# A kernel of slot attention and a GELU feed-forward net: the hand-written order of its start is laid out anew and reaches further

## The chip, the cores and the metric

The kernel runs on one core of one Trainium2 chip. The metric is the time of one execution in device microseconds. The kernel before took 703.89 us, the median of three runs (703.46 to 704.96). Five engines of the core matter here. TensorE (PE in the profile, PEld for its weight loads) does matrix products and transposes; VectorE (DVE) and ScalarE (ACT) do the work element by element; GpSimd (POOL) does some integer additions; SyncE (SP) issues the loads and stores. Each engine takes its instructions strictly in the order of its own queue.

## The reference

Eight batches, eight heads, 576 positions of 64 columns, 32 slots; then a feed-forward net over 4608 tokens with 512 inputs, 2048 hidden columns and 512 outputs.

```python
a = np.exp(phi - np.max(phi, axis=2, keepdims=True))       # softmax over the 576 positions
a = a / (np.sum(a, axis=2, keepdims=True) + 1e-09)
k_m = np.einsum('bhsm,bhsd->bhmd', a, k)                   # 32 slots of keys and of values
v_m = np.einsum('bhsm,bhsd->bhmd', a, v)
scores = scale * np.matmul(q, k_m.transpose(0, 1, 3, 2))
attn = np.exp(scores - np.max(scores, axis=-1, keepdims=True))
attn = attn / (np.sum(attn, axis=-1, keepdims=True) + 1e-09)
x = np.matmul(attn, v_m)                                   # heads side by side: 4608 x 512
h = x @ w_in
g = 0.5 * h * (1.0 + erf(h * inv_sqrt2))
return (g @ w_out).astype(np.float32)
```

## The kernel before

The kernel never forms `x`. For each batch it multiplies the 256 rows of slot values (8 heads of 32 slots) into `w_in` once; the result is `U`, 256 x 2048. The hidden layer is then `h = P U`, with `P` the attention weights of a token over all 256 slots. A batch is two halves of 288 tokens, and the 2048 hidden columns are 16 blocks of 128.

To keep float32's precision, each large product is made of three: an operand is split into a rounded part (`_hi`, a cast) and the remainder (`_lo`, a subtraction on VectorE), and hi x hi, lo x hi and hi x lo are summed. So each operand costs one cast and one subtraction: `U` (pieces `Uh`, `Ul`), the weights `p` (`n_hi`, `n_lo` in batch 0; `ph`, `pl` later), the GELU's output (`gh`, `gl`), and `w_out` (`dE`, `dF`). The casts can stand on VectorE or on ScalarE.

The weights come from memory as 64-bit floats and are decoded on the chip, block by block, 32 half blocks in all: `dB` (two steps on ScalarE, on tiles `y` and `raw`), `dC` and `dS` (VectorE, `y`), `dG` (VectorE, `raw`), `dDi` or `dDo` (GpSimd).

The stages of the start. `phi` of batch 0 is loaded (`Lphi`), its maximum taken (`amax`), exponentiated (`aexp`), and transposed on TensorE (`at`, tiles `pt`, copied by `atc` into `aT`). `slots` multiplies it with keys and values (tile `pk`); `km` scales the sums; `slotsT` transposes them (tile `tn`); `kT` copies them into `k_blocks` and `kT`. In batch 0 the scores are made in three parts (`n_score`, tiles `psc`, the third with half as many tokens), each with maximum, subtraction, exponential, sum, reciprocal and product (`n_max` to `n_mul`, tiles `mx`, `s`, `smx`); `n_T` transposes them back, and `n_hi` and `n_lo` split them into `p_hi` and `p_lo`, of which piece 0 serves the first half of tokens, and pieces 1 and 2 the second. `Up` makes a block of `U` (tile `pu`). `h.0.0.0` is the first hidden block of batch 0's first half, `gelu` its GELU, and `p.0.0` is the first projection, twelve matmuls into the tiles `acc`. Batches 0 and 1 then run through the first eight blocks while the weights are decoded, and batches 2 to 7 come later one after the other, in halves of tokens (`P`, `O`). For batches from 2 on, `phi` is loaded in its other layout as well (`Lphin`, straight into `aT`, which has one buffer), the maximum is brought there through memory (`mw`, `mr`), added (`anat`) and exponentiated. `W` is a filler: a matmul of ones whose result nobody reads.

What sets the order: `START` is a string of pieces, each with its arguments and, behind a colon, the engine of its copy (`d` VectorE, `a` ScalarE). The kernel walks through it and calls one function for each. After its last piece a plan of pieces with due times takes over (`put`, `run`), in a loop over the hidden blocks. At the end every instruction is tied behind the one before it on its engine, so this order is each engine's order. `HOME` gives each big tile its place in the on-chip memory, so a load waits until the last reader of what was there is done. In the page's line numbers, L210 is the helper of all copies, L531 `slots`, L560 `slots_T`, L615 `score_n`, L598 `u_p`, L693 `n_lo`, L855 `hidden`, L882 `gelu_lo`, L895 `products`.

## Time and profile before

| | |
|---|---|
| median of three runs | 703.89 us (703.46 to 704.96) |
| profiled execution, its own time | 704.61 us |
| its span in the trace | 702.8 us |
| mean granted clock of TensorE | 0.981 |
| TensorE busy | 691.1 us, 98% |
| VectorE busy | 388.6 us, 55% |
| ScalarE busy | 298.4 us, 42% |
| GpSimd busy | 46.6 us, 7% |

The rows below come from the profiled execution, in microseconds from the start of its span; 1.8 us of its time lie outside the span. A clock of 1.00 is 2.4 GHz, of 0.50 1.2 GHz. Matmuls follow each other in a pipeline, so the time of a group of them runs from the start of the first to the end of the last, and neighbours overlap.

### The profile page before, as it was taken

The numbers are of one execution on the slowest core, as the hardware profiler recorded it, in microseconds if no ns is written. First come the engines' busy times: TensorE is split into PE (matmuls) and PEld (weight loads), VectorE is DVE, ScalarE is ACT, GpSimd is POOL, SyncE is SP. The second block draws the span as 40 slices with busy tenths as digits, with TensorE's granted clock in tenths as the row PEclk, the third lists the DMA queues.
The fourth block names the chain that finished last, engine by engine and source line by source line (L and its number), as shares of the span: only waits on it lengthen the run. The fifth ranks groups of instructions, "written<-read, shape, count | busy, mean of one in ns | idle before, by whom it ended". The sixth has DMA issues, their size and how long they took to land.

```text
span 702.8 us, 12357 instructions
## 1 busy us (share of the span) xinstructions
PE 691.1 (98%) x4940; PEld 576.6 (82%) x4940; DVE 388.6 (55%) x705; ACT 298.4 (42%) x768; POOL 46.6 (7%) x39
## 2 busy tenths in 40 slices
...
GB/s 318 329 211 172 154 197 62 133 29 212 86 142 117 177 217 23 65 137 159 190 1 32 82 2 31 1 98 1 30 1 31 83 1 31 1 31 0 31 1 45
DMA packets 30716, 64.37 MB, mean 92 GB/s; under 512 B 3780, under 2 KB 8644, under 8 KB 30660
## 3 DMA queue, kind: packets, MB, share of 16 engines
...
q10 hardware_dynamic: 96, 0.13, 0.1%
q14 instruction: 17, 0.14, 0.1%
...
## 4 chain that ended last, share of the span: by engine, by line
PE 94%; DMA 1%; DVE 1%; SPq 0%; ACT 0%; issue 0%
PE acc L895 50%; PE h L855 29%; PE tacc L895 6%; PE pu L598 4%; PE psc L598 1%; PE psc L506 1%; DMA raw<-w_in 1%; PE pk L531 1%; PE x L506 1%; SPq L345 0%; PE pk L506 0%; PE psc L519 0%; PE psc L560 0%; DVE aT L210 0%; PE x L519 0%
## 5 line engine op out<-in xcount | busy, mean ns | idle before, releaser
L855 PE MATMUL h<-p_hi,U 128*128 128x288 f32 x1024 | 203.8, 298 | 0.0
L895 PE MATMUL acc<-wo_hi,gh 128*128 128x512 f32 x512 | 200.6, 392 | 0.0
L895 PE MATMUL acc<-wo_hi,gl 128*128 128x512 f32 x512 | 199.7, 390 | 0.0
L895 PE MATMUL acc<-wo_lo,gh 128*128 128x512 f32 x512 | 199.6, 390 | 0.0
L867 ACT ACTIVATE gf<-h 128x256 f32<-128x256 f32 x192 | 74.0, 387 | 265.0 <-issue 206.4
L855 PEld LDWEIGHTS h<-p_hi,U 128*128 128x128 f32 x1024 | 164.0, 188 | 23.0 <-issue 8.3
L210 DVE CAST gh<-gf 128x512 fp32r<-128x512 f32 x109 | 46.9, 430 | 167.4 <-ACT gf L867 165.3
L895 PEld LDWEIGHTS acc<-wo_hi,gh 128*128 128x128 f32 x512 | 96.5, 188 | 21.1 <-DVE gl L882 3.4
L895 PEld LDWEIGHTS acc<-wo_hi,gl 128*128 128x128 f32 x512 | 96.1, 188 | 21.5 <-DVE gl L882 0.9
L895 PEld LDWEIGHTS acc<-wo_lo,gh 128*128 128x128 f32 x512 | 96.1, 188 | 15.8
L855 PE MATMUL h<-p_lo,U 128*128 128x288 f32 x512 | 108.8, 294 | 0.1
L882 DVE TENSOR_TENSOR gl<-gf,gh 128x512 fp32r<-128x512 f32 x128 | 94.3, 736 | 15.2 <-ACT gh L210 5.7
L855 PEld LDWEIGHTS h<-p_lo,U 128*128 128x128 f32 x512 | 81.4, 188 | 0.6 <-DVE p_lo L693 0.6
L814 DVE TENSOR_TENSOR U<-pu,U 128x512 fp32r<-128x512 f32 (+2 forms) x50 | 40.8, 834 | 42.0 <-ACT U L210 41.8
L869 ACT ACTIVATE tails<-h 128x32 f32<-128x32 f32 x192 | 37.4, 195 | 0.0
L598 PE MATMUL pu<-w_in_sb,kT 64*32 64x512 f32 (+2 forms) x624 | 34.4, 528 | 0.4 <-ACT kT L210 0.4
L210 ACT CAST U<-pu 128x512 fp32r<-128x512 f32 (+2 forms) x42 | 30.4, 759 | 7.4 <-PE pu L598 7.3
L305 POOL TENSOR_TENSOR w_in_sb<-y,raw 128x512 int32<-128x512 int32 x16 | 23.8, 1493 | 43.8 <-DVE y L285 11.8
L305 POOL TENSOR_TENSOR y<-y,raw 128x512 int32<-128x512 int32 x16 | 21.9, 1374 | 56.5 <-DVE y L285 23.9
L272 ACT ACTIVATE y<-raw 128x512 f32<-128x512 f32 x32 | 21.6, 675 | 8.9 <-issue 4.3
L895 PE MATMUL tacc<-wo_hi,gh_t 128*128 128x512 f32 x64 | 25.0, 391 | 0.0
L895 PE MATMUL tacc<-wo_hi,gl_t 128*128 128x512 f32 x64 | 24.9, 389 | 0.0
...
## 6 DMA issues: line engine op xcount, KB each, us to landing
...
raw<-w_out SPq DMA_DIRECT2D x16, 512.0 KB, 5.6
raw<-w_in SPq DMA_DIRECT2D x16, 512.0 KB, 4.5
out<-o SPq DMA_DIRECT2D x16, 512.0 KB, 2.7
...
aT<-phiN SPq DMA_DIRECT2D x6, 512.0 KB, 4.7
...
```

The costliest lines, as they stand in the source:

```text
L210: return e.copy(dst, src) if e is nc.scalar else e.tensor_copy(dst, src)
L272: nc.scalar.activation(y, high.bitcast(F32), AF.Abs, scale=2.0**16)
L305: nc.gpsimd.tensor_tensor(w, y, low, op=ALU.add)
L506: nc.tensor.matmul(pk[32 * j : 32 * j + 32, : 2 * D], st["aT", b][:, c, g, 32 * j : 32 * j + 32], st["kv", b, g, c][:, :, j, :], start=(c ...
L531: nc.tensor.matmul(pk[32 * j : 32 * j + 32, w0 * D : (w0 + n) * D], st["aT", b][:rows, c, g, 32 * j : 32 * j + 32], t[:rows, w0 : w0 + n, ...
L598: nc.tensor.matmul(ps[g][M * j : M * j + M], st["kT", b][rows, t, M * j : M * j + M], moving[j][rows], start=True, stop=True,)
L814: nc.vector.tensor_sub(u[:, ..., 1, :], pu, u[:, ..., 0, :].bitcast(F32))
L855: i = nc.tensor.matmul(h[:, :HS], u[g][w], x[:, g, :], start=(n == 0), stop=(n == 3 * G - 1))
L867: nc.scalar.activation(gf[:, f % 2 * n : f % 2 * n + n], h[:, :n], AF.Gelu)
L869: nc.scalar.activation(t, h[:, n:HS], AF.Gelu)
L882: nc.vector.tensor_tensor(g_of("gl", *k), g_of("gf", *k), g_of("gh", *k).bitcast(F32), op=ALU.subtract)
L895: nc.tensor.matmul(acc, x, w[:, f, :], start=(first and n == 0), stop=(last and n == 2))
```

## The change

`START` grows from 694 pieces to 850 and is written in another order. Before, it ended in the last projections of batch 1's second eight blocks; now it reaches through the first half of batch 2's tokens (`P.2.0.7`, `O.2.0.1`). The plan behind it has the same entries less the pieces already done. `HOME` is unchanged. What each piece computes is unchanged too; the piece `anat` is taken apart into `aadd` (VectorE) and `ax` (ScalarE), which batches from 3 on had already, and the store of a finished pair of output tiles is a piece of its own (`os`) where it was the last step of `o`. The lines that set `far` stand ahead of the walk through `START`, so that pieces of batches 2 and later find them. Which engine makes a copy changes at some pieces: in the program VectorE has 690 instructions where it had 707, ScalarE 775 where it had 756; the others have as many as before.

The diff, of the table only its first and last lines:

```diff
-W.4.3 Lphi.0.0 amax.0.0 aexp.0.0 at.0.0.0 Lphi.0.1 amax.0.1 aexp.0.1 anorm.0 atc.0.0.0:d
...
-h.1.15.1 gelu.1.15.0 pl.2.1 p.1.14 gelu.1.15.1 gh.1.15 amax.3.1 gl.1.15 tg.1.0 p.1.15
+Lphi.0.1 Lphi.0.0 Lwo.0 Lkv0.0.0 Lkv0.1.0 Lq.0.0 W.4.3 amax.0.1 Lwo.1 W.4.13 amax.0.0 Lwi.0
...
+O.2.0.0:a h.2.1.1 O.2.0.1 gelu.2.0.1 gelu.2.1.1 Lkv.5.1.2 gh.2.1.0 gl.2.1.0
@@ -469,10 +480,6 @@
         c = {"tn": b - 1, "pk": 3 if b == 4 else b - 2}[what]
         psc = [(("psc", c, hf), g) for hf in range(2) for g in range(G)]
         return [cut(psc[g], FB - P, FB) for g in ((1, 2) if what == "tn" else (0, 3))]
-
-    def a_nat(b):
-        a_add(b)
-        a_x(b)
 
     def a_x(b):
         x = st["aT", b].rearrange("p c g n -> p (c g n)")[:, : S * G]
@@ -959,11 +966,12 @@
             nc.vector.tensor_add(o, a, st["part", b, j])
         else:
             copy("da"[j % 2], o, a)
-        if f == NF - 1 and j % 2:
-            r = b * S + (j - 1) * P
-            nc.sync.dma_start(
-                out[r : r + 2 * P, :].rearrange("(c p) n -> p c n", p=P), st["o", b, j // 2]
-            )
+
+    def store(b, j):
+        r = b * S + (j - 1) * P
+        nc.sync.dma_start(
+            out[r : r + 2 * P, :].rearrange("(c p) n -> p c n", p=P), st["o", b, j // 2]
+        )
 
     def tail_evict(b):
         o = sb.tile([P, DM], F32, **home(f"to_{b}"))
@@ -985,7 +993,7 @@
     pieces = {
         "Lphi": load_phi, "Lkv": load_kv, "Lkv0": load_kv0, "Lq": load_q,
         "Lwi": lambda f: load_w(0, f), "Lwo": lambda f: load_w(1, f),
-        "Lphin": load_phin, "mw": a_out, "mr": a_back, "anat": a_nat, "aadd": a_add, "ax": a_x, "amax": a_max, "aexp": a_exp, "anorm": a_norm,
+        "Lphin": load_phin, "mw": a_out, "mr": a_back, "aadd": a_add, "ax": a_x, "amax": a_max, "aexp": a_exp, "anorm": a_norm,
         "at": a_T, "atc": a_Tc, "slots": slots, "km": slots_m,
         "slotsT": slots_T, "kT": k_T,
         "n_score": score_n, "n_max": n_max, "n_sub": n_sub, "n_exp": n_exp, "n_sum": n_sum,
@@ -994,10 +1002,13 @@
         "ph": p_hi, "pl": p_lo, "Up": u_p, "Uh": u_h, "Ul": u_l, "U": absorb,
         "W": warm, "dB": dec_b, "dC": dec_c, "dG": dec_g, "dS": dec_s, "dDi": lambda f: dec_d(0, f),
         "dDo": lambda f: dec_d(1, f), "dE": dec_e, "dF": dec_f,
-        "h": hidden, "gelu": gelu, "gh": gelu_hi, "gl": gelu_lo, "p": project, "o": evict,
+        "h": hidden, "gelu": gelu, "gh": gelu_hi, "gl": gelu_lo, "p": project, "o": evict, "os": store,
         "P": project_half, "O": evict_half,
         "tg": tail_split, "tp": tail_project, "to": tail_evict,
     }
+    st.update({("far", "pu", b, f): 1 for b in range(3, B) for f in (4, 12)})
+    st.update({("far", "psc", b, 1): 1 for b in range(3, B)})
+    st.update({k: 1 for k in (("far", "xt", 3), ("far", "pu", 2, 12))})
     done = set()
 
     def do(x):
@@ -1032,7 +1043,7 @@
         put(t + 3, f"mw.{b}")
         put(tn - 1, f"Lphin.{b}")
 
-        put(tn + 1, f"anat.{b}", *(f"aexp.{b}.{g}" for g in range(G)), f"anorm.{b}")
+        put(tn + 1, f"aadd.{b}", f"ax.{b}", *(f"aexp.{b}.{g}" for g in range(G)), f"anorm.{b}")
 
 
     prepare(2, T2, T2 + 5)
@@ -1044,9 +1055,6 @@
     put(t + 13, "slotsT.2", "kT.2")
 
 
-    st.update({("far", "pu", b, f): 1 for b in range(3, B) for f in (4, 12)})
-    st.update({("far", "psc", b, 1): 1 for b in range(3, B)})
-    st.update({k: 1 for k in (("far", "xt", 3), ("far", "pu", 2, 12))})
     for hf, at in ((0, n + 22), (1, n + 26)):
         put(at - 4 if hf == 0 else n + 23, f"Lq.2.{hf}")
         put(at, f"score.2.{hf}", f"sT.2.{hf}.0", f"sT.2.{hf}.1")
@@ -1165,7 +1173,10 @@
         if b < 2:
             behind = [f"p.{step}"]
             if end:
-                behind += [f"o.{b}.{j}.{f}" for j in range(NT)]
+                for j in range(NT):
+                    behind += [f"o.{b}.{j}.{f}"]
+                    if f == NF - 1 and j % 2:
+                        behind += [f"os.{b}.{j}"]
         else:
             behind = [f"P.{step}"]
             if end:
```

How it moves instructions is shown at three places. Numbers behind a name are those of its buffer.

On TensorE, from the first slot sums of batch 0 (`pk`, keys of both groups of heads) to the first two parts of the scores (`psc`). Before:

```order
L531 MATMUL pk_0_144<-kv_0_135,aT_107 32x64 x16
L531 MATMUL pk_0_144<-kvt_0_136,aT_107 32x64 x4
L531 MATMUL pk_1_180<-kv_1_139,aT_107 32x64 x16
L531 MATMUL pk_1_180<-kvt_1_140,aT_107 32x64 x4
L295 MATMUL warm_99<-one 128x128
L560 MATMUL tn_215<-ident,km_201 128x128
L615 MATMUL psc_0_220<-k_blocks,q_0_167 128x2x32 x8
L615 MATMUL psc_1_237<-k_blocks,q_1_169 128x2x32 x8
```

Now:

```order
L306 MATMUL warm_158<-one 128x128
L538 MATMUL pk_0_160<-kv_0_106,aT_128 32x64 x16
L538 MATMUL pk_0_160<-kvt_0_107,aT_128 32x64 x4
L538 MATMUL pk_1_186<-kv_1_110,aT_128 32x64 x16
L538 MATMUL pk_1_186<-kvt_1_111,aT_128 32x64 x4
L567 MATMUL tn_214<-ident,km_207 128x128
L622 MATMUL psc_0_220<-k_blocks,q_0_114 128x2x32 x8
L622 MATMUL psc_1_243<-k_blocks,q_1_136 128x2x32 x8
```

The filler between the slot sums and their transpose `tn` is gone; one stands ahead of the slot sums.

On VectorE, around `p_lo` of batch 0's first half. Before, from the second `U` block's cast on:

```order
L281 TENSOR_SCALAR raw_317<-raw_317 128x512
L285 TENSOR_SCALAR y_343<-y_343 128x512
L210 CAST U_0_339<-pu_1_360 128x2x128
L814 TENSOR_TENSOR U_0_339<-pu_1_360,U_0_339 128x2x128
L634 TENSOR_REDUCE mx_2_388<-psc_2_355 128x8
L639 TENSOR_TENSOR s_2_390<-psc_2_355,mx_2_388 128x256
L281 TENSOR_SCALAR raw_317<-raw_317 128x512
L277 TENSOR_SCALAR y_343<-y_343 128x512
L285 TENSOR_SCALAR y_343<-y_343 128x512
L693 TENSOR_TENSOR p_lo_0_404<-pT_0_374,p_hi_0_403 128x288
L693 TENSOR_TENSOR p_lo_0_404<-pT_1_376,p_hi_0_403 128x288
L210 COPY aT_396<-pt_0_397 128x4x128
```

Now, the rows around the same subtraction:

```order
L288 TENSOR_SCALAR y_341<-y_341 128x512
L296 TENSOR_SCALAR y_341<-y_341 128x512
L646 TENSOR_TENSOR s_1_293<-s_1_293,smx_1_334 128x512
L292 TENSOR_SCALAR raw_240<-raw_240 128x512
L641 TENSOR_REDUCE mx_2_385<-psc_2_328 128x8
L821 TENSOR_TENSOR U_0_364<-pu_0_355,U_0_364 128x2x128
L646 TENSOR_TENSOR s_2_394<-psc_2_328,mx_2_385 128x256
L700 TENSOR_TENSOR p_lo_0_389<-pT_0_369,p_hi_0_388 128x288
L700 TENSOR_TENSOR p_lo_0_389<-pT_1_371,p_hi_0_388 128x288
L322 TENSOR_TENSOR wo_lo<-y_229,wo_hi 128x512
L656 TENSOR_REDUCE smx_2_420<-s_2_394 128x8
L821 TENSOR_TENSOR U_0_364<-pu_1_396,U_0_364 128x2x128
```

The casts of `U` and the copy to `aT` no longer stand here, there are fewer decode steps (`y`, `raw`) ahead of `p_lo`, and a subtraction of `wo_lo` stands behind it.

The third place is around the first GELU, on ScalarE and on SP. On ScalarE, from the copies of batch 1's `aT` to the first GELU (`gf`; the table load is the GELU's). Before:

```order
L210 COPY aT_396<-pt_0_397 128x4x128
L646 ACTIVATE s_2_390<-s_2_390 128x256
L272 ACTIVATE y_435<-raw_372 128x512
L273 ACTIVATE raw_372<-raw_372 128x512
L689 CAST p_hi_1_438<-pT_0_374 128x224
L689 CAST p_hi_1_438<-pT_1_376 128x224
L210 COPY aT_396<-pt_4_426 64x128
L873 ACT_TABLE_LOAD
L873 ACTIVATE gf_0_455<-h_0_0_415 128x288
L689 CAST p_hi_1_438<-pT_2_451 128x64 x2
L549 ACTIVATE km_481<-pk_0_460,rz_448 128x2x64
```

Now:

```order
L221 CAST wo_hi<-y_341 128x512
L221 CAST U_0_364<-pu_1_396 128x2x128
L283 ACTIVATE y_422<-raw_324 128x512
L284 ACTIVATE raw_324<-raw_324 128x512
L283 ACTIVATE y_422<-raw_324 128x512
L284 ACTIVATE raw_324<-raw_324 128x512
L221 COPY aT_428<-pt_0_429 128x4x128 x2
L696 CAST p_hi_1_454<-pT_0_369 128x224
L696 CAST p_hi_1_454<-pT_1_371 128x224
L696 CAST p_hi_1_454<-pT_2_449 128x64 x2
L221 COPY aT_428<-pt_4_459 64x128 x2
L880 ACT_TABLE_LOAD
```

All copies to `aT` are here now, and all of `p_hi` of the second half stands ahead of the table load.

On SP's queue of loads at the same place, from the last loads of batch 1's keys and values on (`raw` is a weight block, `q` batch 1's queries). Before:

```order
L345 DMA kv_1_3_518<-kv 128x512
L345 DMA kv_1_4_548<-kv 64x512
L251 DMA raw_515<-w_in 128x1024
L251 DMA raw_587<-w_in 128x1024
L379 DMA q_0_589<-qT 128x1152
L251 DMA raw_652<-w_in 128x1024
L251 DMA raw_662<-w_out 128x1024
L251 DMA raw_587<-w_out 128x1024
L251 DMA raw_689<-w_in 128x1024
L379 DMA q_1_732<-qT 128x1152
```

Now:

```order
L356 DMA kv_1_4_492<-kv 64x512
L356 DMA kv_1_3_498<-kv 128x512
L262 DMA raw_510<-w_out 128x1024
L262 DMA raw_515<-w_out 128x1024
L390 DMA q_0_527<-qT 128x1152
L262 DMA raw_510<-w_in 128x1024
L445 DMA aT_590<-phiN 128x4x256
L450 DMA aT_590<-phiN 128x1x128
L262 DMA raw_515<-w_in 128x1024
L390 DMA q_1_674<-qT 128x1152
L262 DMA raw_682<-w_in 128x1024
```

The two loads of batch 2's `phi` into `aT` stand ahead of the second `w_in` block of this list and of what follows it.

## Rows read from the trace of the kernel before

**Rows 1.** The page's first part: busy time, share of the span, instructions.

```profile
PE 691.1 (98%) x4940; PEld 576.6 (82%) x4940; DVE 388.6 (55%) x705; ACT 298.4 (42%) x768; POOL 46.6 (7%) x39
```

**Rows 2.** Windows: length, busy time by engine (instructions), granted clock, DMA share, GB/s.

```profile
10.20:34.10 23.90, 21.36 (x246) 17.65 (x234) 18.67 (x41) 11.14 (x26) 6.85 (x5) 0.50 0.96 350
34.10:37.50 3.40, 2.02 (x10) 1.01 (x8) 3.30 (x10) 2.70 (x8) 1.31 (x1) 1.00 0.35 142
37.50:40.90 3.40, 3.39 (x44) 2.53 (x45) 1.73 (x8) 2.64 (x6) 1.29 (x1) 0.50 0.34 117
47.33:82.90 35.57, 35.57 (x293) 26.67 (x286) 35.02 (x70) 28.68 (x56) 10.59 (x8) 1.00 0.41 150
47.33:698.00 650.67, 650.67 (x4510) 544.18 (x4503) 354.79 (x627) 270.04 (x706) 33.65 (x24) 1.00 0.24 77
```

**Rows 3.** The chain that ended last, its longest pieces: start, length, what.

```profile
82.86 2.78 PE acc L895 x12
...
687.82 10.89 PE tacc L895 x48
```

**Rows 4.** Timeline of PE: start, length, work, [idle before <-releaser].

```profile
13.90 0.45 PE L560 MATMUL tn<-ident,km 128*128 128x128 f32 x1
15.07 7.06 PE L615 MATMUL psc<-k_blocks,q 128*128 128x64 f32 x32 [0.72 <-ACT k_blocks L210]
...
33.57 0.76 PE L855 MATMUL h<-p_hi,U 128*128 128x288 f32 x2
...
36.86 0.30 PE L423 MATMUL pt<-ident,phi 128*64 128x128 f32 x1 [1.12 <-DVE aT L210]
...
39.96 0.85 PE L855 MATMUL h<-p_hi,U 128*128 128x288 f32 x2
...
43.59 1.43 PE L531 MATMUL pk<-kv,aT 128*32 128x128 f32 x40
...
47.33 0.50 PE L895 MATMUL acc<-wo_hi,gh 128*128 128x512 f32 x1
```

**Rows 5.** Timeline of DVE, same columns, with one row from 79 to 84.

```profile
18.75 0.69 DVE L634 TENSOR_REDUCE mx<-psc 128x16 f32<-128x512 f32 x1 [0.67 <-PE psc L615]
...
28.27 0.42 DVE L210 CAST U<-pu 128x256 fp32r<-128x256 f32 x1
...
30.06 0.74 DVE L281 TENSOR_SCALAR raw<-raw 128x512 uint16<-128x512 uint16 x1
30.58 0.46 DVE L285 TENSOR_SCALAR y<-y 128x512 int32<-128x512 int32 x1
...
33.97 0.81 DVE L693 TENSOR_TENSOR p_lo<-pT,p_hi 128x288 fp32r<-128x288 f32 x2
34.70 0.68 DVE L210 COPY aT<-pt 128x512 f32<-128x512 f32 x1
...
36.53 0.28 DVE L210 COPY aT<-pt 64x128 f32<-64x128 f32 x1
...
39.43 0.95 DVE L693 TENSOR_TENSOR p_lo<-pT,p_hi 128x64 fp32r<-128x64 f32 x4 [1.12 <-ACT p_hi L689]
...
42.47 0.72 DVE L311 TENSOR_TENSOR wo_lo<-y,wo_hi 128x512 fp32r<-128x512 f32 x1
...
43.81 1.10 DVE L882 TENSOR_TENSOR gl<-gf,gh 128x512 fp32r<-128x512 f32 x1 [0.29 <-ACT gh L210]
...
82.25 0.69 DVE L882 TENSOR_TENSOR gl<-gf,gh 128x512 fp32r<-128x512 f32 x1
```

**Rows 6.** Timeline of ACT, same columns, around the first transpose of slots.

```profile
13.10 0.31 ACT L549 ACTIVATE km<-pk,rz 128x64 f32<-128x64 f32 x1 [1.73 <-PE pk L531]
...
14.44 0.53 ACT L210 COPY k_blocks<-tn 64x128 f32<-64x128 f32 x2
```

**Rows 7.** Timeline of SP's queue, same columns, from 36 to 46 us.

```profile
40.80 0.38 SPq L251 DMA_DIRECT2D raw<-w_in  x1
```

**Rows 8.** DMA issues: what, engine, count, KB each, median us to landing.

```profile
raw<-w_in SPq DMA_DIRECT2D x16, 512.0 KB, 4.5
```

More of the change, by code (lines that the diff above doesn't have):

```diff
@@ new lines @@
+gelu.0.10.1 dG.14.0 gh.0.9:a h.0.11.0 gh.0.10:a dE.13 gl.0.9 h.0.11.1 dF.13 gelu.0.11.0
+Up.0.12.2 Lkv.2.0.3 gelu.0.11.1 dC.14.0 Lwo.14 dB.15.0 p.0.9 dS.14.0 Lphi.3.0 dDi.14 dC.15.0
+Lkv.2.0.2 Uh.0.12:a dS.15.0 Lkv.2.0.0 Ul.0.12 h.0.12.0 gl.0.10 h.0.12.1 gh.0.11 dG.15.0 p.0.10
+gelu.0.12.1 dDi.15 dB.15.1 gelu.0.12.0 dG.15.1 dB.14.1 gl.0.11 h.0.13.0 dG.14.1 h.0.13.1
+gh.0.12:d amax.3.1 Up.0.14.2 dC.14.1 p.0.11 dC.15.1 Uh.0.14:a dS.14.1 gelu.0.13.0 Ul.0.14
+gelu.0.13.1 dS.15.1 gl.0.12 dDo.15 amax.3.0 h.0.14.0 h.0.14.1 dDo.14 p.0.12 dE.14 Lkv.2.1.1
@@ new lines @@
+Lkv.2.1.2 gh.0.13:a Lkv.2.1.0 gelu.0.14.1 gl.0.13 Lkv.2.1.3 gelu.0.14.0 dF.14 p.0.13 gh.0.14
+aexp.3.1 dE.15 dF.15 gl.0.14 h.0.15.0 h.0.15.1 gelu.0.15.0 p.0.14 gelu.0.15.1 gh.0.15:d
+gl.0.15 aadd.2 p.0.15 ax.2 aexp.3.0 o.0.2.15 h.1.8.0 o.0.0.15 Lkv.3.0.1 h.1.8.1 Lkv.2.1.4
+Lkv.2.0.4 mw.3 Up.1.12.4 gelu.1.8.1 gelu.1.8.0 Lphi.4.0 gh.1.8 Lkv.2.0.1 h.1.9.0 gl.1.8
+Uh.1.12 h.1.9.1 o.0.3.15 o.0.1.15 p.1.8 gelu.1.9.1 Ul.1.12 mr.3 gelu.1.9.0 Lphi.4.1 Lkv.3.0.0
+anorm.2 slots.2.0 slots.2.1 Lkv.3.0.4 h.1.10.0 km.2.0 Lphin.3 gh.1.9:d km.2.1 h.1.10.1 gl.1.9
@@ new lines @@
+os.0.1 gelu.1.10.0 Lkv.3.0.2 amax.4.0 h.1.11.0 gelu.1.10.1 os.0.3 Lkv.3.0.3 slotsT.2 kT.2:d
+h.1.11.1 score.2.0 gelu.1.11.1 gh.1.10:a p.1.9 sT.2.0.1 Lq.2.1 gelu.1.11.0 sT.2.0.0 max.2.0
+sub.2.0 aadd.3 h.1.12.0 Up.2.0.4 gl.1.10 h.1.12.1 gelu.1.12.0 p.1.10 gelu.1.12.1 exp.2.0
+gh.1.11:a sum.2.0 h.1.13.0 inv.2.0 h.1.13.1 gl.1.11 p.1.11 mul.2.0 gelu.1.13.1 gelu.1.13.0
+pT.2.0 gh.1.12:a ph.2.0:d gl.1.12 Uh.2.0:d p.1.12 gh.1.13 pl.2.0 Ul.2.0 h.1.14.0 gl.1.13
+h.1.14.1 gelu.1.14.0 h.1.15.0 gelu.1.14.1 h.1.15.1 gelu.1.15.0 gh.1.14:a h.2.0.0 Lq.3.1
```

121 lines of the change are left out of this document (57 added, 64 removed).

## The prediction, made before the changed kernel was run

> **What bounds the kernel now.** I read the busy table first. TensorE is busy 691.1 of 702.8 us, 98% [rows 1], so little can be won except where it is idle or slow. Busy time alone doesn't say that it runs at its peak, so I read next the stretches with the granted clock. From 47.33 us, where the first projection starts, to 698 us it is busy in every microsecond, at full clock [rows 2]. Then the pace inside that stretch, from the chain of work that ended last: the last 48 matmuls, the tail's projection, take 10.89 us, 227 ns each; the twelve of an early projection, at 82.86, take 2.78 us, 232 ns each [rows 3]. The early part runs at the pace of the end: there is no hidden stall behind the 47.33 us mark. A new order of the same matmuls can therefore win only ahead of that mark, and can lose anywhere behind it.
>
> Ahead of the mark TensorE loses time in two ways. From 10.2 to 34.1 us and again from 37.5 to 40.9 us the granted clock is 0.50, 1.2 GHz [rows 2]. And it waits. The last long wait before the steady part is one of VectorE: the 64-row transposes of `phi` stand still until 36.86 us for a copy of `aT` on VectorE [rows 4]. VectorE takes its instructions in order. The maximum over the first part of the scores is released at 18.75 us; from there VectorE works almost without a break until `p_lo` of the first half of batch 0 (33.97), the `aT` copies (34.70, 36.53), and `p_lo` of the second half (39.43, after 1.12 us of waiting for ScalarE's `p_hi`) [rows 5]. On TensorE `h` of the first half starts at 33.57, of the second at 39.96 [rows 4]. So the start of the steady part hangs on how much stands in VectorE's queue between 18.75 and 40.4 us.
>
> **The change, part by part.** *Warm-up matmul out of the way of the first transpose.* Before, a filler stands between the first slot sums and their transpose, which starts at 13.90 [rows 4]. The scaled sums that the transpose reads are ready at 13.10 + 0.31 = 13.41 [rows 6]. Now no filler stands there (one stands ahead of the slot sums, which wait for their loads), and the transpose can start at about 13.5: 0.4 us. The copies to `k_blocks` (14.44) follow 0.54 us behind the transpose, as before; ScalarE now has a `wo_hi` cast in front of them, which falls into that 0.54 us. The scores then start at 14.67 instead of 15.07 [rows 4, 6], and with them everything that VectorE waited for at 18.75. Term 1: -0.4 us.
>
> *VectorE's queue.* From the first maximum to `p_lo` of the first half there stood 34 instructions, now 25: two casts of `U` (0.42 each), one subtraction of `U` (much the same), two steps on `raw` (0.52 from one start to the next) and four on `y` (0.46 each) have gone elsewhere or behind it [rows 5]. By these durations that is 0.84 + 0.42 + 1.04 + 1.84 = 4.14 us; since neighbours overlap by about 0.1 us, between 3.2 and 4.1. This `p_lo` ended at 33.97 + 0.81 = 34.78 and comes at about 30.8. It brings `h` of the first half ahead of batch 1's transposes, as the new PE order wants it, but does not by itself bring the steady part.
>
> That is set by `p_lo` of the second half, ended at 39.43 + 0.95 = 40.38. Up to it go out two `U` casts (0.84), both `aT` copies (0.68 + 0.28), one step on `raw` (0.52) and one on `y` (0.46); two `wo_lo` subtractions come in (0.72 each) [rows 5]. Net 2.78 - 1.44 = 1.3 us less. The 1.12 us that it waited for `p_hi` goes too: ScalarE now has these casts ahead of the GELU's table load. Term 2: -2.4 us. With term 1 this `p_lo` ends at 40.38 - 0.4 - 2.4 = 37.6 us.
>
> *From there to the first projection.* Before: 47.33 - 40.38 = 6.95 us, of which 0.5 us at half clock (until 40.9). If the level changes stay where they are, 40.9 - 37.6 = 3.3 us of the same work now runs at half clock, 2.8 us more, which costs 1.4 us. Term 3: +1.4. The first projection starts at 37.6 + 6.95 + 1.4 = 45.9, 1.4 us sooner. The order of TensorE gives some of it back: while the half clock runs it has the 64-row transposes of batch 1 and its first slot sums behind it already, which stood between 36.86 and 39.96 [rows 4]; I put 0.3 us of those 3.1 on that. Sum: -1.7 us.
>
> *Cover for it.* The first `gl` must be there 0.5 us into the projection. Up to it VectorE has one instruction more than before (56 against 55), two of the added three being the 0.72 us subtractions, so it ends not before 43.81 + 1.10 - 0.4 + 0.7 = 45.2 us, or 44.1 without the lost wait [rows 5]: in time for 45.6, and a floor that would stop a gain beyond about 2.9 us. Behind it VectorE is full: 35.02 of 35.57 us up to 82.9 [rows 2], and it delivers the eighth `gl` at 82.25 + 0.69 = 82.94, when the eighth projection, begun at 82.86 [rows 3], is running. A TensorE 1.7 us ahead would catch up with it there, if the queue were the same. It isn't: between the first and the eighth `gl` stand 59 instructions instead of 74; at 35.02 us for 70 instructions, 0.5 us each, that is 7.5 us less. So VectorE isn't late next.
>
> *ScalarE* takes the copies over. Ahead of its first GELU it has eleven more instructions; at 0.43 us each (11.14 us for 26 in the stretch from 10.2 to 34.1) that is 4 to 5 us, and it was idle 12.8 of those 23.9 us [rows 2]. Between the first and the eighth GELU its count hardly changes (67 against 68), and it was busy 28.68 of 35.57 us there. Cost nothing; if its queue is caught by one late operand, the price is the whole gain (rival 2).
>
> *Second halves of kv behind one more load of phi.* 288 KB at the 350 GB/s of that stretch [rows 2] are 0.8 us. Below: nothing. Above: 0.8 us on TensorE, as no filler stands before these sums any more. I take nothing, since the wait would fall ahead of a chain that VectorE holds.
>
> *Behind the mark.* The third batch's first half is now pinned as well, output stores have names of their own, copies of `part` go to ScalarE. The matmuls are the same in number. With TensorE full and no wait to take away, this can bring nothing; what it can cost is in rivals 2 and 3.
>
> The profiled execution took 704.61 us for a span of 702.8; less 1.7 that is 702.9. It lies 0.7 us above the median of the runs, 703.89, which becomes 702.2.
>
> **The rivals.** *1. The clock rises earlier.* If `h` of the first half and batch 1's transposes follow each other closely enough, the stretch from 37.5 on is granted full clock. Then term 3 is nothing, the first projection starts at 37.6 + 6.95 = 44.6, and the gain is 2.8 us, just what the first `gl` allows: 701.1. For it: full clock was granted from 34.1 to 37.5, between two stretches at half [rows 2], behind transposes that followed each other closely. Against it: the new order still has waits for `p_lo` and for copies at that place.
>
> *2. The gain is eaten before 47 us.* The clock may as well stay at half for one more stretch like that from 37.5 to 40.9: 3.4 us at half rate cost 1.7 us, and the gain is nothing. Or a ScalarE queue that is 4 to 5 us fuller holds `gh` of the second projection back. 703.8. For it: the fillers that stood at 13 and 22 us have gone to the front, so TensorE is idle more often between 13 and 26 us; and the clock fell at 37.5 behind a stretch in which TensorE was busy for 2.02 of 3.40 us [rows 2].
>
> The Trainium skill has a rule for this, in "TensorE: Matmul & The Clock Gate", section "Part 1: The HAM clock gate": the throttled state is the default, and it is activity that releases it. The trace agrees so far, with 0.50 behind the stretch with the waits and 1.00 from 47.33 on. By that rule taking fillers out of waits speaks against the change, and the time would be rival 2's.
>
> *3. Slower: the load of phi for batch 2 blocks the queue of loads.* On SP it now stands ahead of `w_in` 6 and `w_in` 7. It writes `aT`, which is free only when the last slot sums of batch 1 are done: before at 43.59 + 1.43 = 45.02 [rows 4], now at about 43.3 us. Before, `w_in` 6 was issued at 40.80 [rows 7], and such a load lands 4.5 us later [rows 8], at 45.3. Now it goes out at 44.4 behind 576 KB (1.6 us at 350 GB/s) and lands at 49 to 50.5. ScalarE comes to its first decode step at about 48.3 (estimate: first GELU at 37.8, then 9.7 us of queue at 0.43 us each and 0.8 us of waits); behind that step stand the GELUs of `h` 3 and `gh` of the third projection. TensorE has the second projection, 2.7 us, as cover. From a landing at about 51 us on, each further microsecond is one of TensorE's. A load that is 3 to 4 us later than I reckon, at this and the next blocked place, makes 705.5. For it: VectorE's queue waits behind the same operand. Against: the queues carried 350 GB/s when full.
>
> *4. The order doesn't matter here:* if the half clock, not VectorE, paces the scores and transposes up to 34 us, only term 1 arrives: 703.5. I count it with rival 2.
>
> **How the numbers follow.** Forecast (gain 1.0 to 2.4, time 701.5 to 702.9) 0.42; rival 1 0.21; rivals 2 and 4 0.23; rival 3 0.14. The likeliest time is 702.2. The range reaches from a gain a little over the floor, 700.2, to rival 3's 705.5. About 0.2% (1.4 us) is what a measurement of this kernel can tell from no change: faster by that is rival 1 and 0.7 of the forecast, 0.21 + 0.29 = 0.50; within it 0.13 + 0.23 = 0.36; slower 0.14.
>
> **What would show it.** The first projection at 45 to 46 us instead of 47.33; scores at 14.7; `p_lo` of the second half ended before 38; `aT` copies on ScalarE; TensorE full from the first projection to the end, with the same 650.7 us behind it up to the same matmul. A first projection where it was, or a wait of TensorE behind it, would make the forecast wrong; so would a clock that is granted at other times, which shows in the stretches from 30 to 45 us.

## The result: slower by 8.9 us

The changed kernel takes 712.81 us (median of four runs, 712.47 to 713.7), the kernel before 703.91 us beside it: a ratio of 1.0126 [1.0109, 1.0144], slower by 8.9 us. The forecast was 702.2, and the range ended at 705.5. The profiled execution took 712.92 us, its span 711.1 us, against 702.8 before.

The busy table of the kernel after, same columns as [rows 1]:

```profile
PE 693.8 (98%) x4940; PEld 575.4 (81%) x4940; DVE 379.7 (53%) x688; ACT 305.9 (43%) x787; POOL 45.2 (6%) x39
```

TensorE's share is 98% as before, so this table hides the loss. Where it lies shows in stretches cut at the same piece of work: the first projection, the 41st, the 121st. After, in the columns of [rows 2] (length; PE, PEld, DVE, ACT, POOL busy; granted clock; DMA share; GB/s):

```profile
17.00:25.60 8.60, 8.11 (x104) 7.21 (x105) 7.98 (x17) 5.14 (x11) 3.82 (x3) 0.50 1.04 367
25.60:29.60 4.00, 3.51 (x43) 2.33 (x42) 3.15 (x8) 3.43 (x10) 1.29 (x1) 0.50 1.03 412
29.60:30.20 0.60, 0.60 (x18) 0.38 (x3) 0.60 (x3) 0.60 (x3) 0.00 (x0) 0.74 0.98 396
30.20:37.50 7.30, 4.91 (x64) 3.50 (x62) 7.20 (x23) 7.14 (x18) 1.45 (x1) 1.00 0.68 218
...
43.72:261.18 217.46, 212.35 (x1583) 170.62 (x1577) 143.87 (x253) 124.76 (x270) 32.66 (x24) 1.00 0.43 140
...
261.18:664.47 403.29, 403.29 (x2715) 339.27 (x2713) 190.81 (x339) 143.70 (x421) 0.00 (x0) 1.00 0.15 45
```

The same two pieces of work in the kernel before:

```profile
47.33:256.79 209.46, 209.46 (x1585) 170.41 (x1577) 152.02 (x267) 119.77 (x258) 33.65 (x24) 1.00 0.43 136
256.79:656.45 399.66, 399.66 (x2714) 337.71 (x2713) 189.84 (x338) 143.54 (x421) 0.00 (x0) 1.00 0.16 51
```

The sum of the spans: the first projection starts 47.33 - 43.72 = 3.6 us sooner; the next forty take 217.46 - 209.46 = 8.0 us more, of which TensorE shows 217.46 - 212.35 = 5.1 us idle; the eighty behind them take 403.29 - 399.66 = 3.6 us more without a moment of idleness; the rest of the span takes 0.3 more. -3.6 + 8.0 + 3.6 + 0.3 = 8.3 us. The eighty are the surprise: same matmuls, same order, clock 1.00 in both, nothing waits, and yet 0.9% slower.

TensorE's timeline after, beside [rows 4] (start, length, work, idle before and releaser):

```profile
13.10 3.65 PE L622 MATMUL psc<-k_blocks,q 128*128 128x64 f32 x16 [0.67 <-ACT k_blocks L221]
...
29.82 0.56 PE L862 MATMUL h<-p_hi,U 128*128 128x288 f32 x2
...
36.66 0.53 PE L862 MATMUL h<-p_hi,U 128*128 128x288 f32 x2
...
43.72 0.50 PE L902 MATMUL acc<-wo_hi,gh 128*128 128x512 f32 x1
...
50.29 0.45 PE L605 MATMUL pu<-w_in_sb,kT 64*32 64x128 f32 x16 [0.67 <-DVE sT L719]
50.67 0.51 PE L902 MATMUL acc<-wo_hi,gh 128*128 128x512 f32 x1
...
63.40 0.45 PE L605 MATMUL pu<-w_in_sb,kT 64*32 64x128 f32 x16 [1.17 <-DVE sT L719]
```

What TensorE waited for between 43 and 262 us after (in total, times, longest; the same stretch before has none):

```profile
PE pu L605 <- DVE sT L719: 1.8, 2, 1.2
PE pk L513 <- DMA kvU<-kv: 1.0, 1, 1.0
PE h L862 <- ACT tails L883: 0.9, 1, 0.9
PE psc L605 <- ACT kT L221: 0.8, 1, 0.8
PE h L862 <- ACT tails L876: 0.3, 1, 0.3
PE acc L902 <- DVE gl L889: 0.2, 1, 0.2
PE acc L902 <- DVE o L966: 0.2, 1, 0.2
```

These sum to 5.2 us. The first two are waits for `sT`, the transposes of batch 1's scores on VectorE, at 50.29 and 63.40 us. What made the first, on ScalarE and on VectorE after:

```profile
46.23 0.67 ACT L283 ACTIVATE y<-raw 128x512 f32<-128x512 f32 x1 [0.97 <-DMA raw<-w_in]
...
47.70 0.62 ACT L221 CAST gh<-gf 128x512 fp32r<-128x512 f32 x1
```

```profile
35.82 0.98 DVE L700 TENSOR_TENSOR p_lo<-pT,p_hi 128x224 fp32r<-128x224 f32 x4
...
48.35 0.69 DVE L889 TENSOR_TENSOR gl<-gf,gh 128x512 fp32r<-128x512 f32 x1 [1.95 <-ACT gh L221]
...
49.30 0.84 DVE L719 STREAM_TRANSPOSE sT<-psc 128x288 f32<-128x288 f32 x2
```

ScalarE meets a decode step (`y<-raw`) whose load hasn't landed; the cast `gh` behind it comes later; VectorE waits 1.95 us for that cast and has `sT` behind it in its queue; TensorE's `pu` waits for `sT`. The second goes back to the next load of `w_in`. The chain of work that ended last, from 40 to 64.5 us after, of which these are pieces, runs from that load through the queues of ScalarE and VectorE to the matmul that waited, with no other transfer in it:

```profile
42.48 7.28 DMA raw<-w_in
...
50.42 0.67 ACT raw L284
...
55.64 0.52 ACT gh L221
...
56.18 1.60 DVE gl L889
...
62.40 0.86 DVE sT L719 x2
...
63.40 0.45 PE pu L605 x16
```

### The profile page after: what moved, and what is told of

Same layout as the page of the kernel before. It is cut to its first block, busy times and chain, and to the rows that moved or that the text cites. A ratio compares the mean times of both kernels' runs of the same rounds, so it can differ in the third digit from the quotient of the medians.

```text
span 711.1 us, 12357 instructions
## 1 busy us (share of the span) xinstructions
PE 693.8 (98%) x4940; PEld 575.4 (81%) x4940; DVE 379.7 (53%) x688; ACT 305.9 (43%) x787; POOL 45.2 (6%) x39
## 4 chain that ended last, share of the span: by engine, by line
PE 89%; DMA 5%; DVE 2%; ACT 2%; SPq 1%; issue 1%; ACTq 0%; DVEq 0%
PE acc L902 47%; PE h L862 28%; PE tacc L902 6%; PE pu L605 4%; DMA kv<-kv 1%; DMA q<-q 1%; DMA raw<-w_in 1%; PE psc L605 1%; DMA kvU<-kv 1%; DMA aT<-phiN 1%; PE psc L513 1%; PE pk L538 1%; PE x L513 1%; PE psc L622 0%; DVE wo_lo L322 0%
## 5 line engine op out<-in xcount | busy, mean ns | idle before, releaser
L221 DVE CAST gh<-gf 128x512 fp32r<-128x512 f32 x103 | 43.6, 423 | 170.7 <-ACT gf L874 162.5
L889 DVE TENSOR_TENSOR gl<-gf,gh 128x512 fp32r<-128x512 f32 x128 | 90.3, 706 | 30.6 <-ACT gh L221 21.6
L876 ACT ACTIVATE tails<-h 128x32 f32<-128x32 f32 x192 | 37.5, 195 | 0.0
L221 ACT CAST U<-pu 128x512 fp32r<-128x512 f32 (+2 forms) x44 | 28.9, 690 | 8.0 <-PE pu L605 7.9
L292 DVE TENSOR_SCALAR raw<-raw 128x512 uint16<-128x512 uint16 x32 | 26.9, 849 | 6.8 <-ACT raw L284 6.6
L902 PE MATMUL tacc<-wo_hi,gh_t 128*128 128x512 f32 x64 | 25.3, 395 | 0.0
```

The lines of the kernel that those rows point to most:

```text
L221: return e.copy(dst, src) if e is nc.scalar else e.tensor_copy(dst, src)
L292: nc.vector.tensor_single_scalar(low, high, 0x8000, op=ALU.bitwise_and)
L876: nc.scalar.activation(t, h[:, n:HS], AF.Gelu)
L889: nc.vector.tensor_tensor(g_of("gl", *k), g_of("gf", *k), g_of("gh", *k).bitcast(F32), op=ALU.subtract)
L902: nc.tensor.matmul(acc, x, w[:, f, :], start=(first and n == 0), stop=(last and n == 2))
```

## The experiments

`START` decides two things. It is the order of work, and it is the order in which tiles are first asked for: `HOME` only names a buffer for each big tile, and the pool gives a buffer its address when that name is first used. The new order so moves buffers. Before, all five buffers of `U` start at a multiple of 256 bytes; after, at 64, 0, 128, 64 and 64 bytes past one. Theory 1: the addresses make the lasting slow pace, and the new order by itself makes the waits. Its rival: the order makes both.

**Order and addresses apart.** Four kernels. "Old addresses" is this edit, which asks for each buffer once, in the old order of first use, before `START` is walked; "new addresses" is the same with the new order of first use.

```diff
+PLACE = """
+phi nm sm aT rz mx smx U0 U4 kv0 U3 kv7 U2 q tails wy0 km wy1 sT pT U1 kv6 kv1 kv2 kv5 p_hi0
...
+    for tag in 'acc0 acc2 acc1 acc3'.split():
+        ps_acc.tile([P, FB], F32, tag=tag, name=f"first_{tag}")
+    for tag in PLACE.split():
...
+            sb.tile([P, 2], F32, tag=tag, name=f"first_{tag}_{x}", **kw)
```

The new order at old addresses:

> The changed kernel's order, with every tile of on-chip memory and every accumulator bank at the address it had before (tags are touched once in the old order of first use). Theory 1 (placement): the changed order also moved the tiles, and the 128x512 matmuls of the steady part run 230 ns instead of 228 for that reason; then the part behind the 40th projection, 461 to 711 us in the trace of the changed kernel and 3.6 us longer there than before for the same matmuls, comes back, and some 1.5 us of pace ahead of it: 707 to 708.5. Theory 2 (the pace hangs on the order of work, not on addresses): 712 to 713.5.

Measured 708.48 us, 1.0073 [1.0057, 1.0088]. The old order at new addresses:

> The order of before, with the tiles and accumulator banks where the changed kernel has them. Theory 1 (placement): slower by the same 3.6 to 5 us, 707.5 to 709, with matmul pace 230 ns from the first projection to the end. Theory 2 (order): 703.5 to 704.5 and 228 ns.

Measured 708.91 us, 1.0073 [1.0059, 1.0086]. The eighty projections in windows, first of the new order at old addresses, then of the old order at new ones:

```profile
259.60:659.20 399.60, 399.60 (x2713) 337.71 (x2713) 190.75 (x339) 143.64 (x421) 0.00 (x0) 1.00 0.15 46
```

```profile
257.30:660.60 403.30, 403.30 (x2714) 339.21 (x2713) 189.74 (x338) 143.68 (x421) 0.00 (x0) 1.00 0.16 51
```

The pace goes with the addresses and not with the order. By the ratios the addresses cost (0.0126 - 0.0073) x 703.9 = 3.7 us under the new order and 0.0073 x 703.9 = 5.1 under the old. The rest of the loss, 5.1 us, is order.

**The head of the order alone.** The next pair splits the order at the first projection, `p.0.0`, both at old addresses: the new order up to it and the old behind, and the reverse. (Pieces that the first part has done are left out of the second.)

```diff
-... Up.0.3.1 dE.4 dS.4.0 p.0.0 Uh.0.3 dF.4 gelu.0.2.0 dG.4.0 dB.5.0 ...
+... Up.0.3.1 dE.4 dS.4.0 p.0.0 gh.0.1:a gl.0.1 dG.4.0 dF.4 gelu.0.2.1 ...
```

> The new order up to and with the first projection, the order of before behind it (for what is left), tiles at the addresses of before. Theory A (the start's gain is real and is lost to waits that the new order makes behind it: VectorE's transposes of scores at 50 and 62 us, loads behind the early load of phi, late ACT and DMA at 158 to 166 us): first projection at 43.7, steady pace 228 ns, no wait over 1 us behind: 700 to 701.5. Theory B (VectorE cannot keep up with an earlier start in any order): the 3.6 us are given back by the eighth projection: 703 to 704.5.

Measured 701.56 us, 0.9972 [0.9961, 0.9982]: a gain of 2.0 us, the size that the prediction gave to the whole change (1.7). Its windows from the first projection on:

```profile
43.57:253.76 210.19, 209.74 (x1584) 170.34 (x1577) 150.92 (x266) 119.27 (x256) 33.48 (x24) 1.00 0.41 135
253.76:653.40 399.64, 399.64 (x2714) 337.76 (x2713) 189.76 (x338) 143.53 (x421) 0.00 (x0) 1.00 0.16 51
```

TensorE is idle for 0.45 us of the first 210.19 (209.46 before), and the eighty projections take their old time. The reverse, old up to `p.0.0` and new behind:

> The order of before up to and with the first projection, the new order behind it, tiles at the addresses of before. Theory A (the new order behind the first projection makes its own waits, 5 us of them): 707.5 to 709.5. Theory B (those waits come from the earlier start alone): first projection at 47.3 and nothing lost at 50 and 62 us, so at most the 2.2 us of idle time at 158 to 262 us: 704 to 706.

Measured 712.59 us, 1.0129 [1.0104, 1.0153], several us above both forecasts. The two parts don't add up: a wait of 1.9 us of `psc` for a `U` subtraction stands at the seam, where the new order counts on work that the old one hasn't done, and first and second projection lie 9.0 us apart (50.67 - 43.72 = 7.0 after, 5.8 before). The trace also has a stretch of half clock from 51.6 to 55.0 us, behind that wait, with TensorE busy for all of it. How the rest comes about wasn't followed.

**Which addresses.** Two halves of theory 1, one run each: the four `acc` banks alone back at their old places, and the operands' memory alone (the edit above without, and with only, its second loop).

> The changed kernel with only its four accumulator banks put back where they were before (first use in the order acc0, acc2, acc1, acc3); the rest of on-chip memory as in the changed kernel. If the banks set the pace: 40th to 120th projection in 399.7 us, matmuls of 128x512 every 227.2 ns in the mean. If the addresses of operands do: 403.3 us and 229.5 ns, as in the changed kernel.

713.44 us, the eighty projections 403.30 us: the banks change nothing.

> The other half: the changed kernel with the operands' memory laid out as before and the accumulator banks as in the changed kernel (first use acc3, acc2, acc0, acc1). If the banks set the pace: 403.3 us from the 40th to the 120th projection; if the operands' addresses do: 399.7 us.

707.86 us and 399.68: it is the operands. As a counter-test the old order with another order of banks:

```diff
+    for tag in 'acc0 acc1 acc2 acc3'.split():
+        ps_acc.tile([P, FB], F32, tag=tag, name=f"first_{tag}")
```

> The kernel before with its accumulators in banks 0, 1, 2, 3 in sequence (the two that the later batches use lie side by side, as in the changed kernel, but in banks 0 and 1 rather than 2 and 3). If neighbouring accumulator banks are what costs pace: 403 us from the 40th to the 120th projection; if it is the distance to the banks of h, or the operands' addresses: 399.7 us.

704.59 us, 399.67: no effect. Inside the trace after, the starts of two `h` matmuls in a row, averaged by the buffer of `U` they read (batches 3 to 7, worked out from all of them), point to a single suspect:

```
buffer   bytes past a multiple of 256   ns from h to h   acc to acc behind it, ns
U1         0                            130.77           226.6
U0        64                            132.85           230.0 to 231.0
U3, U4    64                            132.81, 132.89   (as U0)
U2       128                            133.36           (as U0)
before, all five: 0                     130.76 to 130.79 226.6 to 227.4
```

So the new order and layout, with five small tiles asked for at other points so that each `U` starts at a multiple of 256 bytes:

```diff
+PLACE = """
+phi nm U0 U4 kv0 U3 kv7 q U2 aT tails wy0 km wy1 sm rz mx smx U1 sT kv3 pT kv1 kv5 kv4 kv6 kv2
...
```

> The changed kernel's order and layout, but five small tags of sums and maxima (nm, sm, rz, mx, smx) are allocated elsewhere, so that every U tile starts at 0 modulo 256 (in the changed kernel one of five does). If the start of U is what the changed layout did to the pace: 399.7 us from the 40th to the 120th projection, 708 to 709 us. If something else in the layout did: 402 to 403.3 us, 711 to 713.

Measured 707.9 us, 1.0061 [1.0043, 1.0078], and in its trace:

```profile
261.80:661.50 399.70, 399.70 (x2715) 337.74 (x2714) 190.74 (x339) 143.62 (x421) 0.00 (x0) 1.00 0.15 46
```

Where five small tiles stand, and with them the tiles behind, decides the whole 3.6 us. What lies behind it is less clear. Three more kernels, the first two with one run each. Old order with 64 unused bytes ahead of the first `U` (`U` and `p` both 64 past):

```diff
-phi nm sm aT rz mx smx U0 U4 ...
+phi nm sm aT rz mx smx pad64 U0 U4 ...
```

> The kernel before, unchanged in order, with 64 bytes of unused memory in each partition ahead of the first U tile: U, p and all behind them lie at 64 modulo 256 instead of 0. If it is U's own start modulo 256 that costs pace: 402 to 403.5 us from the 40th to the 120th projection and h matmuls every 132.9 ns in batches 3 to 7 for every U tile. If it is U's start against that of p (in the changed kernel U lies at 64 or 128 and p at 0): 399.7 us and 130.8 ns, since both move together.

705.5 us, the eighty projections 400.97: `h` to `h` slows to 132.4 ns, but `acc` to `acc` stays at 226.8. Neither forecast came: 1.3 of the 3.6 us. With the 64 bytes ahead of `p` only (`U` at 0):

```diff
-... kv1 kv2 kv5 p_hi0 ...
+... kv1 kv2 kv5 pad64 p_hi0 ...
```

> The same 64 bytes put in ahead of the first p tile instead, so that U stays at 0 modulo 256 and p lies at 64. If U's own start costs: 399.7 us and 130.8 ns. If the start of U against that of p costs, or p's own: 402 us or more.

703.57 us, 400.33 for the eighty: between the two forecasts again, with `h` to `h` at 131.5 ns. And the new head with every big operand at a multiple of 256, `w_in`, `wo`, `gh` and `gl` too, which lie 192 bytes past one in both kernels:

```diff
+    const.tile([P, 16], F32, name="shift")
...
-phi nm sm aT rz mx smx U0 U4 ...
+phi aT U0 U4 ... p_lo3 cols nm sm rz mx smx
```

> The kernel with the new order up to the first projection and the old one behind, with all big tiles at 0 modulo 256: U and p as before, and now also w_in, w_out's two parts and gh, gl, which lay at 192 (the small tiles of sums and maxima have gone to the end). If the start of the acc matmuls' operands counts as that of U does: the 128x512 matmuls fall below 227.2 ns, by up to 6 ns as U's tiles did, and the time from 701.6 by up to 9 us. If only U's start counts, or if 192 is as good as 0: 701.0 to 702.2, with 399.7 us from the 40th to the 120th projection.

704.18 us, 1.0007 [0.9998, 1.0015] against 701.56 of the same order unshifted; the eighty projections 402.01 us, `acc` to `acc` 228.8 ns (the edit leaves out the order of the `acc` banks, which changed nothing above). This too is outside both forecasts. So "a multiple of 256 for each" is not the rule: aligning more operands made it worse. And `h` to `h` slows to 132.1 ns here, though `U` and `p` start at multiples of 256 as before, so `U`'s own start isn't the cause by itself. What counts seems to be how the operands of `h` and of `acc` matmuls, which take turns, lie to one another; that is not shown, and the mechanism stays open.

**Where the order loses.** Three borders between new and old order, all at old addresses, and moves of single pieces. The border at `p.1.6`, the 15th projection:

> New order up to the projection p.1.6 (451 pieces, as many as the old order has up to there, all but ten the same), old order behind it, tiles at the old addresses. Theory A (each stretch of the new order makes its own waits): the losses of 1.5 us up to p.1.6 stay, those behind it (3.7 us of idle and slower work from 130 to 260 us) go: 703.5 to 704.8. Rival (the waits at 157, 164 and 225 us follow from what the earlier new order leaves undone): 706 to 708.5.

704.01 us, 1.0002 [0.9993, 1.001]: the head's gain is gone. The border at `p.0.13`, the 22nd:

> New order up to the projection p.0.13, old order behind it, tiles at the old addresses. If the waits at 157, 164 and 225 us come from the pieces behind p.0.13 (preparing batches 2 and 3): 703.8 to 705. If the middle stretch (p.1.6 to p.0.13) makes the loss: 706.5 to 708.5.

702.75 us, 0.9985 [0.9974, 0.9995], below the forecast. So between the first projection and the 22nd the new order loses about 1 to 2 us (by this border 0.9, with intervals that overlap; by the earlier one 2.1, so a border has a price of its own), and behind it 0.0073 + 0.0015 of 703.9, 6.2. For the first part there are two suspects, `phi`'s second load for batch 2 in the queue of loads (rival 3) and the decode step in front of `gh`:

```diff
-... km.1.1 Lphin.2 gh.0.0:d ...
+... km.1.1 gh.0.0:d ...
...
-... o.0.1.7:a gl.1.0 ...
+... o.0.1.7:a Lphin.2 gl.1.0 ...
```

> As the kernel with the new order up to p.1.6, but the early load of batch 2's phi (Lphin.2) is put where the order before had it, behind the copies of batch 0's first sums. Theory (that load waits for aT and holds w_in 6 and later blocks behind it on SP, so ScalarE's decode and the GELUs queued behind it are late): w_in 6 goes out before 40 us, ScalarE has no wait of 1 us for raw at 45 to 50 us, and the time from the first to the second projection falls from 7.0 us to 6 or less; 0.8 to 1.2 us less than that kernel's 704.0: 702.8 to 703.3. Rival (the queue of loads is full there anyway, the load behind takes the place): same time within 0.3 us.

703.32 us, 0.9999 [0.9988, 1.001], not told apart from its parent in time. In the trace the fourth projection to the fifth takes 7.3 us where it took 8.3. All three traces without the early load show 7.2 to 7.3 there; of the eight that keep it in the new order, six show 8.3 to 8.5, but two 7.2 and 7.3, the uncut order at old addresses among them. So the load's price there is 1.0 us, and not in every execution. The first to the second stays at 7.0 us, for which I had forecast 6 or less. Then the decode step as well:

```diff
-... dG.4.0 dB.5.0 Ul.0.3 dDi.4 gelu.0.2.1 gh.0.1:a ...
+... dG.4.0 Ul.0.3 dDi.4 gelu.0.2.1 gh.0.1:a dB.5.0 ...
```

> As mid_late, with the first decode step of w_in block 5 (dB.5.0, on ScalarE) put behind the cast gh.0.1 instead of ahead of a GELU and that cast. Theory (the decode waits 1.05 us for a load that lands at 46.7 us, and GELU, gh, gl and VectorE's transpose of scores stand behind it): gl.0.1 at 46.5 to 47 instead of 48.9 us, no wait of TensorE at 50 us, first to second projection 6.0 to 6.3 us instead of 7.1: 702.2 to 702.7 against 703.3. Rival (VectorE's own queue holds the transposes): same within 0.3.

702.44 us, 0.9987 [0.9977, 0.9997], in time not told apart from its parent either; first to second projection 6.2 us, as forecast, where traces of the new order without the move show 6.4 to 7.1. ScalarE's timeline of the two kernels, without and with the second move:

```profile
46.81 0.67 ACT L272 ACTIVATE y<-raw 128x512 f32<-128x512 f32 x1 [1.05 <-DMA raw<-w_in]
...
48.29 0.62 ACT L210 CAST gh<-gf 128x512 fp32r<-128x512 f32 x1
```

```profile
45.16 0.63 ACT L210 CAST gh<-gf 128x512 fp32r<-128x512 f32 x1
46.50 0.68 ACT L272 ACTIVATE y<-raw 128x512 f32<-128x512 f32 x1 [0.71 <-DMA raw<-w_in]
```

The wait for the load stays, but `gh` is out before it. The head alone without the early load:

> As head_new (new order up to the first projection, old order behind, old addresses), without the early load of batch 2's phi, which goes back to its old place in the old part. If that load's queueing costs in this kernel too: w_in 6 lands earlier, ScalarE's 0.57 us wait for it at 50 us goes, 700.7 to 701.3. Rival: the load of w_in 6 is hidden here, since the casts stand ahead of the decode: 701.6 as head_new, within 0.4.

701.42 us, 0.9971 [0.996, 0.9981]: within the noise of the head alone (701.56), so undecided. For the part behind `p.0.13`, the new order at old addresses shows these waits of TensorE, and its queue of loads the reason for the second:

```profile
158.50 0.53 PE L875 MATMUL h<-p_hi,U 128*128 128x288 f32 x2 [0.88 <-ACT tails L896]
...
164.91 1.74 PE L518 MATMUL pk<-kvU,aT 128*32 128x128 f32 x56 [1.02 <-DMA kvU<-kv]
```

```profile
155.10 0.33 SPq L361 DMA_DIRECT2D kv<-kv  x1
155.70 1.16 SPq L351 DMA_DIRECT2D kvw<-kv  x2
158.01 0.43 SPq L361 DMA_DIRECT2D kvU<-kv  x1
```

The last piece of batch 2's keys and values stands behind loads of batches 2 and 3 that wait for memory, and goes out at 158.01. Moved ahead of them:

```diff
-... Lkv.2.1.3 gelu.0.14.0 ... gh.1.8 Lkv.2.0.1 h.1.9.0 ...
+... Lkv.2.1.3 Lkv.2.0.1 gelu.0.14.0 ... gh.1.8 h.1.9.0 ...
```

> The new order at the old addresses (as new_place_old, 708.5 us) with one load moved on SP: the last piece of batch 2's keys and values (Lkv.2.0.1) goes out behind the other pieces of that tile, at about 145 us, instead of behind the loads for batch 3 that wait for memory until 155 us. Theory (batch 2's slot sums wait 1.0 to 1.9 us for it at 164 us): that wait goes, 706.8 to 707.6, and the single times spread less. Rival (another load or aT itself is as late): 708 to 709.

707.75 us, 1.0048 [1.0032, 1.0064]: the wait is gone, and the median moves by 0.7, within the two intervals. All four moves together (this load, `phi`'s, the decode step, and the order of two GELUs, `gelu.1.8.0` first, so that ScalarE's table load isn't in front of `tails` at 158):

> The same with three more moves of single pieces in the new order: the early load of phi back to its old place, the decode step dB.5.0 behind the cast gh.0.1, and the GELU of the first half of h 1.8 ahead of that of the second half (so that the GELU's table load starts when the first half is there and not the second). Theory (the later order's loss is a handful of such places): 1.4 for the load, 0.7 and 0.9 as in mid_late and mid_late_db, 0.9 for the wait at 157 us, from 708.5 to 704.5 (704 to 705.3). Rival (the loss is spread over the order, each wait removed shows the next): above 706.

705.29 us, 1.0023 [1.0012, 1.0034], at the upper end of the forecast. (0.0073 - 0.0023) x 703.9 = 3.5 of the order's 5.1 us are taken back. In its trace TensorE is 2.7 us ahead of the kernel before at the 25th projection and 1.0 behind at the 41st, with named waits of only 0.8 (`psc` for `kT`) and 0.3 (`tails`) there. The rest is in small pieces: in the new order at old addresses, 52 pairs of neighbouring matmuls start 0.3 to 0.6 us apart where 41 did before. What makes these stays open.

## Why the prediction was wrong

By the ratios: the head of the order gives 0.0028 x 703.9 = 2.0 us; the order behind it costs 0.0073 + 0.0028, 7.1 us; the addresses cost 3.7. -2.0 + 7.1 + 3.7 = 8.8 of the 8.9. These are steps along one row of kernels, so that they add up is no test of them; taken in another order they differ (the addresses cost 5.1 under the old order). The prediction had the first, and nothing for the other two.

*Terms 1 and 2, right in mechanism, each off in size.* Scores began at 13.10 us (forecast 14.67). Of these 1.97 us, 0.92 is that the slot sums began at 8.91 instead of 9.83, where they waited for a load of keys (the lines below, before and after); over the traces that start varies just as much in either order (8.3 to 10.6 us in six whose order up to `p.0.0` is the old one, 8.4 to 10.8 in fourteen with the new one, a piece or two moved in some). From the slot sums to the scores 1.05 us went (0.5 to 1.6 over the traces), where term 1 had 0.4. `p_lo` of the second half ended at 35.82 + 0.98 = 36.80 (forecast 37.6); from the first scores to there it took 23.7 us instead of 25.3, so 1.6 less where term 2 had 2.4 (1.5 to 2.7 over the traces). `h` of the two halves starts at 29.82 and 36.66, before at 33.57 and 39.96 [rows 4]. The step from [rows 5], that the start hangs on VectorE's queue, held; that the two misses, one too small and one too large, cancel in part is luck. The floor that the first `gl` sets (44.1 to 45.2) was near: it ended at 44.57, and TensorE waited 0.2 us for it.

```profile
9.83 0.78 PE L531 MATMUL pk<-kv,aT 128*32 128x64 f32 x32 [2.43 <-DMA kv<-kv]
```

```profile
8.91 0.65 PE L538 MATMUL pk<-kv,aT 128*32 128x64 f32 x32
```

*Term 3: its price was right, but the new order doesn't decide whether it falls due.* It put the clock's changes where one trace had them. There the clock rose at 34.1 and fell again from 37.5 to 40.9 [rows 2]; after, it rose at about 29.9, behind 8.6 us with TensorE busy for 8.11 and 4.0 with 3.51, at half clock, and stayed at 1.00, even from 30.2 to 37.5 where TensorE was busy for 4.91 of 7.30 us. The first projection came at 43.72, where rival 1 had 44.6. But the second stretch at half clock is in two of the six traces with the old start and in four of the fourteen with the new one, and the mean granted clock of the unchanged kernel before lies anywhere from 0.976 to 0.988 in 99 runs of it. The new order at old addresses has that stretch (columns of [rows 2]):

```profile
31.40:34.80 3.40, 1.86 (x23) 1.12 (x25) 3.38 (x9) 3.38 (x11) 0.06 (x1) 1.00 0.68 255
34.80:38.20 3.40, 3.40 (x46) 2.61 (x34) 2.55 (x8) 2.65 (x5) 2.31 (x2) 0.50 0.45 119
```

From the end of `p_lo` to the first projection the new start takes 8.3 us in these four traces and 6.9 to 7.1 in the other ten, against the forecast's 6.95 + 1.4 and rival 1's 6.95. So the forecast and rival 1 are two outcomes of the same start, and that the profiled execution shows rival 1's is luck. The first rise came at 31.0 to 34.9 us in the six and at 29.5 to 32.8 in the fourteen. By the rule of the Trainium skill that I set against this change ("TensorE: Matmul & The Clock Gate", "Part 1: The HAM clock gate"), that activity releases the throttle, taking fillers out of waits would have made rival 2 come; the traces don't bear that out, for the fillers went and the clock rose no later. The 3.6 us between the two first projections overstate the gain: in the six traces the first projection starts at 45.2 to 47.3 us, in the fourteen at 42.9 to 45.7. The head alone, timed, gave 2.0 us (1.3 to 2.7 by its interval), against the forecast 1.7.

*"So VectorE isn't late next", the first step that failed.* I counted instructions between `gl`s and took their sum for their time. The first time VectorE wasn't late by its own work; it was late because it stood 1.95 us for a cast of ScalarE, and then the transposes `sT`, not a `gl`, were what TensorE waited for (1.8 us in two waits). The second time it began `gl` at 56.18, behind a late cast again, and then 6.2 us of its own queue stood between that and `sT` at 62.40.

*ScalarE: "Cost nothing", failed too.* The price that I had left to rival 2, one late operand, came true: a decode step, standing 0.97 us for its load, in front of `gh`. Moving that one piece shortened first to second projection by 0.8 us in the trace.

*Rival 3, right about the load, wrong about where it costs.* The load of `w_in` went out at 42.48 (forecast 44.4) and landed at 49.76 (forecast 49 to 50.5). By the rival's reckoning only a landing behind about 51 us costs time; this one came before that, and the chain from it still ends in the wait at 63.40, 1.17 us, through `gh`, `gl` and `sT`. With the early load away, the trace gained 1.0 at that place, not 3 to 4.

*"Behind the mark ... this can bring nothing; what it can cost is in rivals 2 and 3", the costly step.* TensorE had been full from 47.33 on [rows 2], so each late operand there is a full loss, and the rivals looked only at 50 us. The dearest part, 6.2 us, lies behind the 22nd projection: a load of keys behind loads of a later batch (a wait of 1.0), a table load in front of `tails` (0.9), a `kT` copy (0.8), and many short gaps, whose cause stays open.

*Addresses: no step at all.* "The matmuls are the same in number" stood for "the same in time". The pace in [rows 3] was taken as a property of the matmul, and 232 ns was read as the same as 227. It is one of the layout too, and 3.7 us of the 8.9 are that.
